# One hand-written issue order replaced by another in a fused adaLN, dilated local attention and token-MLP block

## The chip, the cores and the metric

The kernel runs on one core of a Trainium2 chip. The metric is device time in microseconds (us) of one execution. A second number appears in what follows: the span of the profiled execution, from the first instruction of the program to the end of the last, which is a little shorter than the time of the same execution.

## What is computed

x has 2048 positions of 512 numbers in bf16. Six rows come from a conditioning vector: shifts, scales and gates for two halves.

```python
sa, ca, ga, sb, cb, gb = rows of (silu(c) @ w_mod)            # 6 rows of 512
h = layernorm(x) * (1 + ca) + sa
x = x + ga * attention(h, A_wqkv, A_wo)
h = layernorm(x) * (1 + cb) + sb
x = x + gb * token_mlp(h)
# attention: 32 heads of 16; position s sees s, s-2, ..., s-14 (8 keys, dilation 2), softmax, then @ wo
# token_mlp: layernorm again, then gelu(h^T @ w1 + b1) @ w2 + b2 over the 2048 positions, F = 1792
```

The second half mixes positions: its first product sums over all 2048 positions, its second gives 2048 positions back.

## The kernel before

The positions are cut into 16 tiles of 128, and the tiles into five chunks of 2, 4, 4, 4 and 2 tiles (chunks 0 to 4). Every operation of the program is first recorded in a graph with a name, and then issued in an order that is written out by hand, the string ORDER. Its words are the names. A letter behind a name picks the engine where there are several: `a` ScalarE (ACT), `d` VectorE (DVE), `p` GpSimd (POOL), `s` the queue of SyncE (SP); `q` runs a matmul as four column strips of 32, `n` leaves out an optional extra matmul. `fill:n` issues n dummy 128-column matmuls. Each engine works through its own part of the list strictly in this order, and waits where an input is not there yet. A buffer from a pool (6 banks of PSUM, 4 `big` tiles for products, 5 `vD` tiles) goes to the operation that asks next in the list, and is the one that was freed earliest in the list, so the order also sets who waits for which buffer. All instructions carry the same line in the profile (L143, a wrapper), so groups are told apart by their tiles.

The names, for a chunk c and a tile t:

- `ld_...` are loads on the SP queue; `ld_x_4_14` brings tiles 14 and 15, `ld_wmod2` and `ld_wrow0..3` the weights of the conditioning rows, `ld_w1_...` and `ld_w2_...` those of the token MLP.
- `ln1s_t`, `ln1v_t`, `rstd1_c`, `nb1_c`, `n1_t`: statistics, reciprocal deviation, negative scaled mean (a tiny DVE operation) and norm of the first layernorm. The same with 2 and 3 in place of 1 for the second and third; there `ln2q_t` is the sum of squares on ACT, and `h3_t` is the third norm, which feeds the token MLP.
- `xt_t`: DMA transposes of two normed tiles for chunks 2 to 4.
- `wsc_k_j`: one quarter of a weight matrix scaled by 1 + ca, once. `qkv_c_kj` are the projections (k = 0, 1, 2 for q, k, v), and `ev_c_kj` moves a result out of PSUM to SBUF.
- `halo_v_c`, `halo_k_c` copy the last 16 positions of a chunk in front of the next.
- `qk_c_j` (DVE): elementwise products of q with the eight shifted k; `red_c_j` (PE) sums them over the head dimension into the PSUM tile psL. `max_c` (DVE), `sub_c` (PE), `exp_c` (ACT), `esum_c` (PE), `rcp_c` (ACT) and `smB_c` (DVE) are the softmax. `a2_c_j` and `vd_c_j` are DMAs that bring the weights and the shifted values in place. `pv_c_j` (DVE) multiplies them, `pvacc_c_j` (PE) sums, `oev_c_j` (ACT) brings the sum to SBUF.
- `wo_t` (PE): the output projection with x added; `x1_t` moves it to SBUF and sums it.
- `aff_t` (DVE): the second half's scale and shift, two instructions.
- `mlp1_l_f_s` (PE): pieces of the first token product for feature tile f from position tile s on, started before later tiles exist; `park_l_f` (ACT or DVE) puts a partial sum aside. `gelu_f` and `mlp2_t` follow, then `fin_t` and `st_out_t`.
- `modrow0`, `mrows0`, `st_row0`, `ld_row0` (and 1): the conditioning rows, sent through DRAM to be copied to all partitions; `woq_s` scales wo by ga.

What a step's DVE product looks like, and what the norms may run on:

```python
nc.vector.tensor_tensor(pv(), a2sb.unsqueeze(2).to_broadcast([P, 2, 4, C]), ..., op=ALU.mult)
G.add_any([("act", 0.8, lambda: nc.scalar.activation(dst, src, ACT.Identity, scale=r_, bias=n_)),
           ("dve", 0.42, lambda: nc.vector.tensor_scalar(dst, src, r_, n_, op0=ALU.mult, op1=ALU.add)),
           ("pool", 0.8, lambda: nc.gpsimd.tensor_scalar(dst, src, r_, n_, op0=ALU.mult, op1=ALU.add))],
```

The numbers in such a list were for the making of an order; with ORDER written out they set nothing.

Of the kernel before, what the change touches and what calls it, by code (L numbers as in the profile page):

```python
# [218 lines left out]
a2_3_0:s a2_3_1:s a2_3_3:s n2_4:a qkv4_00:q oev2_2:a rstd3_0 aff2 pvacc2_1 oev2_1:a wo6:q wo9:q wo7:q aff4 nb3_0  # L219
ln3s2:d ev4_02:a ln3s3:a ln3v3 h3_1:p wo8:q a2_3_2:s ev4_00:a ln3v2 ld_w2_0 ln3s4:d rstd3_2 x1_9:a ln3s5:a h3_0:p  # L220
mlp1_0_6_0:q x1_7:a ln3v4 x1_8:a h3_3 mlp1_0_1_0:q h3_2 mlp1_0_6_2:q mlp1_0_1_2:q pv3_1 mlp1_0_5_0:q ln3v5 ev4_10:a
ld_w1_0_896 x1_6:a mlp1_0_3_0:q mlp1_0_3_2:q ln2q7 pvacc3_1 rstd3_4 mlp1_0_5_2:q oev3_1:a mlp1_0_2_0:q pv3_0
mlp1_0_2_2:q nb3_4 h3_4:a mlp1_0_0_0:q mlp1_0_0_2:q h3_5:a mlp1_0_0_4:q qk4_0 ln2q8 ln2q6 park0_0:a ln2q9 mlp1_0_6_4:q
mlp1_0_2_4:q mlp1_0_1_4:q park0_1:a pv3_2 mlp1_0_5_4:q vd3_3 pvacc3_0 oev3_0:a mlp1_0_3_4:q ld_w2_1 park0_2:a pv3_3
red4_0 pvacc3_2 oev3_2:a mlp1_0_4_0:q qk4_1 pvacc3_3 ld_w1_0_1152 mlp1_0_4_2:q mlp1_0_4_4:q rstd2_6 oev3_3:a wo12:q
halo_v4:p vd4_2 vd4_3 nb2_6 n2_9:a qk4_2 n2_7:d qk4_3 wo10:qn red4_1 ld_w1_0_1408 n2_6:a vd4_1 n2_8:a aff6 red4_2
red4_3 max4 park0_3:a ln3s8:d ln3s6:d x1_12:a ln3v8 wo11 vd4_0 ln3s9:d mlp1_0_7_0 ld_w2_3 park0_4:a ln3v6 mlp1_0_7_2
park0_5:a ln3v9 x1_11:a ln2q12 mlp1_0_8_0 mlp1_0_8_2 park0_6:a wo13:n ln3s7:a ln3v7 sub4 mlp1_0_10_0 mlp1_0_9_0 x1_13:d
exp4 rstd3_6 nb3_6 esum4 mlp1_0_8_4 ln2q13 mlp1_0_10_2 mlp1_0_10_4 mlp1_0_9_2 rcp4 mlp1_0_7_4 h3_8:d rstd2_12
mlp1_0_12_0 mlp1_0_12_2 mlp1_0_12_4 smB4 a2_4_1:a a2_4_0:s mlp1_0_9_4 a2_4_2:s h3_9:d a2_4_3:a h3_7:d nb2_12 h3_6:p  # L230
mlp1_0_7_6 ln2q11 park0_7:a x1_10:d mlp1_0_8_6 ld_w1_0_1664 ln2q10 park0_8:a n2_13:p mlp1_0_9_6 park0_9:a n2_12:d aff12
rstd2_10 mlp1_0_10_6 park0_10:a ln3s13 pv4_2 nb2_10 ld_w1_1_0 pv4_1 mlp1_0_11_0 mlp1_0_11_2 mlp1_0_11_4 mlp1_0_12_6
pv4_0 mlp1_0_11_6 ld_w1_1_640 inj1_6:qn pv4_3 pvacc4_0 pvacc4_1 n2_11:a mlp1_0_13_0:q pvacc4_2 pvacc4_3 n2_10:a
mlp1_0_13_2:q park0_11:a mlp1_0_13_4 oev4_0:a oev4_2:a aff10 ln3s10:a wo14 inj1_3:n ln3s11:d ln3v11 x1_14 ln2s14 wo15
x1_15 mlp1_0_13_6 ln2v14 ln3s12 ln3v10 ln2s15 rstd2_14 nb2_14 ln2v15 n2_14:d rstd3_10 aff14 rstd2_15 nb2_15 inj1_4:qn
park0_12:a mlp1_1_3_6 park0_13:a mlp1_1_6_6 inj1_1:n mlp1_1_1_6 n2_15:p mlp1_1_4_6 inj1_0:n mlp1_1_0_6 nb3_10 h3_10:a
mlp1_1_4_10 mlp1_1_3_10 ln3s14:d ld_w2_4 mlp1_1_0_10 ln3v14 rstd3_12 h3_11:a mlp1_1_6_10 inj1_5:n mlp1_1_5_6
mlp1_1_5_10 rstd3_14 mlp1_1_1_10 aff15 nb3_12 ln3s15:d ln3v15 h3_12:p nb3_14 park1_0:+ h3_13:p rstd3_15 nb3_15 inj1_2:n
mlp1_1_2_6 ld_w1_1_896 h3_14:p h3_15:a ld_w1_2_0 park1_1:+ mlp1_1_2_10 park1_2:+ mlp1_1_7_10 park1_3:+ park1_4:+
park1_5:+ mlp1_1_8_10 mlp1_1_10_10 park1_6:+ padd1_7 padd1_10 gelu10 padd1_8 mlp1_1_9_10 padd1_9 gelu9 mlp1_2_4_11  # L240
mlp1_2_4_14 mlp1_2_1_11 mlp1_2_1_14 padd2_1 padd2_4 gelu7 mlp1_2_0_11 mlp1_2_0_14 padd2_0 gelu0 mlp1_2_2_11 gelu4 gelu8
mlp1_2_2_14 ld_w1_1_1408 mlp1_2_3_11 mlp1_2_3_14 padd2_3 gelu3 ld_w1_2_640 mlp1_2_6_11 padd2_6 gelu6 padd2_2 gelu2
mlp1_2_5_11 mlp1_1_11_10 padd1_11 mlp1_2_5_14 padd2_5 gelu1 gelu11 mlp1_1_12_10 ld_w2_5 ld_w2_7 mlp1_1_13_10 gelu5
mlp2_0_0 padd1_12 gelu12 mlp2_0_0b ld_w2_2 ld_w2_9 ld_w2_13 ld_w2_11 padd1_13 gelu13 mlp2_0_0c mlp2_6_0 mlp2_4_0 gsc
fin0_0 st_out0_0 fin4_0 st_out4_0 mlp2_8_0 fin8_0 mlp2_3_0 fin3_0 mlp2_2_0 fin2_0 st_out2_0 mlp2_1_0 fin1_0 mlp2_7_0
st_out3_0 fin6_0 st_out6_0 fin7_0 mlp2_10_0 fin10_0 st_out7_0 mlp2_11_0 mlp2_5_0 st_out1_0 fin5_0 st_out5_0 mlp2_14_0
fin11_0 st_out10_0 st_out11_0 ld_w2_15 fpre mlp2_9_0 mlp2_13_0 fin14_0 st_out14_0 st_out8_0 mlp2_12_0 fin9_0 st_out9_0
# [830 lines left out]
```

## Time and profile before

| what | us |
|---|---|
| median of 3 runs (lowest, highest) | 199.72 (199.3, 200.41) |
| the profiled execution | 199.64 |
| its span | 197.9 |
| granted TensorE clock, mean | 0.999 of full speed |

The page of the profile gives busy time by engine over the span, then groups of instructions. PE is TensorE's matmuls, PEld its weight loads, DVE is VectorE, ACT ScalarE, POOL GpSimd; SPq and ACTq are the sequencers of SP and ACT when they issue DMAs. A row of the timeline reads: start, duration, engine, line, operation, out<-in, shapes, count, and in brackets the engine's idle time before it and what ended it. Matmul ends are modelled, so TensorE can read busy while it works below its rate. Busy shares are means over stages with different limits, so the stages are looked at one by one.

### The profile page before, as it was taken

How to read it: one execution, taken by the hardware profiler on the slowest of the kernel's cores; microseconds unless marked ns; L12 is line 12 of the kernel's file. 1: busy time of each engine (PE TensorE's matmuls, PEld its weight loads, DVE VectorE, ACT ScalarE, POOL GpSimd, SP SyncE). 2: the span in 40 equal slices, each digit the busy share in tenths (PEclk: the TensorE clock that was granted, in tenths of full speed). 3: DMA queues.
4: the chain of work that ended last, by engine and by line, in shares of the span. 5: the costliest groups of instructions: out<-in, count | busy, mean ns of one | idle time of the engine just before them, and what ended most of it. 6: DMA issues, size and time to landing. Idle time of an engine off the chain costs nothing.

```text
span 197.9 us, 5606 instructions
## 1 busy us (share of the span) xinstructions
PE 187.8 (95%) x2348; PEld 101.9 (51%) x2358; DVE 157.5 (80%) x222; ACT 127.8 (65%) x305; POOL 18.5 (9%) x45
## 2 busy tenths in 40 slices
...
GB/s 171 325 358 321 219 227 164 156 57 260 230 223 285 236 191 215 105 159 298 40 332 227 76 209 143 156 241 233 329 224 325 74 0 53 39 44 53 172 53 53
DMA packets 53893, 36.02 MB, mean 182 GB/s; under 512 B 24428, under 2 KB 50668, under 8 KB 53868
## 3 DMA queue, kind: packets, MB, share of 16 engines
...
## 4 chain that ended last, share of the span: by engine, by line
PE 64%; ACT 19%; DVE 5%; DMA 4%; SPq 3%; issue 3%; ACTq 0%; DVEq 0%
PE psS L143 63%; ACT junk L143 4%; DMA vD<-v_sb 3%; SPq L143 3%; ACT xx L143 2%; ACT v_sb L143 2%; ACT h L143 2%; DVE big L143 2%; PE psL L143 2%; ACT q_sb L143 2%; ACT k_f L143 2%; DVE h L143 1%; ACT o_sb L143 1%; DMA c_t<-in_c_dram 1%; ACT lsb L143 1%
## 5 line engine op out<-in xcount | busy, mean ns | idle before, releaser
L143 PEld LDWEIGHTS <-wst 128*128 128x128 bf16 (+1 forms) x584 | 35.6, 101 | 33.0 <-issue 2.8
L143 PE MATMUL psS<-h,wst 128*32 128x512 bf16 (+1 forms) x358 | 50.5, 379 | 0.6 <-issue 0.2
L143 DVE TENSOR_TENSOR big<-q_sb,k_f 128x4096 bf16<-128x4096 bf16 (+1 forms) x20 | 36.6, 1857 | 0.1
L143 DVE TENSOR_TENSOR big<-a2sb,vD 128x4096 bf16<-128x4096 bf16 (+1 forms) x20 | 36.5, 1858 | 0.0
L143 PE MATMUL psS<-hT,w_qkv 128*32 128x512 bf16 (+1 forms) x576 | 29.6, 344 | 0.3 <-ACT o_sb L143 0.3
L143 DVE SCALAR_TENSOR_TENSOR h<-psS,bcol,rows_bc 128x512 f32<-128x512 f32 (+2 forms) x17 | 12.1, 710 | 22.1 <-PE psS L143 20.6
L143 PEld LDWEIGHTS <-w_qkv 128*32 128x32 bf16 (+1 forms) x618 | 22.1, 107 | 14.1 <-issue 0.5
L143 PE MATMUL psS<-gT,big 128*128 128x512 bf16 x110 | 24.7, 379 | 0.1
L143 PEld LDWEIGHTS <-big 128*128 128x128 bf16 x144 | 12.1, 98 | 13.8 <-DMA big<-in_w_mod_dram 0.5
L143 PE MATMUL psS<-woq,o_sb 128*32 128x512 bf16 (+1 forms) x207 | 16.7, 379 | 0.5 <-ACT o_sb L143 0.5
L143 ACT ACTIVATE gT<-psS,bcol 128x512 bf16<-128x512 f32 x14 | 9.0, 686 | 8.3 <-DVE psS L143 8.2
L143 POOL TENSOR_SCALAR h<-xx,rs,nb 128x512 bf16<-128x512 bf16 x9 | 7.0, 785 | 72.7 <-DVE nb L143 33.9
L143 DVE TENSOR_TENSOR psS<-psS,gT 128x512 f32<-128x512 f32 x14 | 9.3, 695 | 5.0 <-PE psS L143 5.0
L143 PE MATMUL psS<-hT,wst 128*32 128x512 bf16 (+2 forms) x135 | 11.7, 355 | 0.1
L143 ACT ACTIVATE h<-xx,nb,rs 128x512 bf16<-128x512 bf16 x15 | 11.6, 812 | 0.0
L143 DVE TENSOR_TENSOR h<-h,xx 128x512 bf16<-128x512 f32 (+2 forms) x17 | 11.1, 653 | 0.6
L143 PEld LDWEIGHTS <-group 128*32 128x32 bf16 x288 | 7.8, 96 | 7.2 <-issue 2.7
L143 DVE BATCH_NORM_STATS2 st<-xx 128x6 f32<-128x512 bf16 x12 | 8.0, 682 | 4.3 <-DMA xx<-in_A_x_dram 4.2
L143 DVE TENSOR_TENSOR h<-h,rows_bc 128x1024 bf16<-128x1024 bf16 (+2 forms) x16 | 10.9, 689 | 0.4
L143 ACT ACTIVATE junk<-xx,sums 128x512 bf16<-128x512 bf16 x14 | 10.1, 722 | 1.6 <-DVE xx L143 1.4
L143 ACT ACTIVATE v_sb<-psS,qvb 128x512 bf16<-128x512 f32 (+1 forms) x20 | 11.0, 597 | 0.0
L143 PEld LDWEIGHTS <-ident 128*32 128x32 bf16 (+2 forms) x242 | 7.1, 99 | 7.4 <-issue 2.8
...
## 6 DMA issues: line engine op xcount, KB each, us to landing
...
xx<-in_A_x_dram SPq DMA_DIRECT2D x6, 256.0 KB, 8.0
...
```

Of the source, the lines that this page charges most:

```text
L143: r = fn(*a, **k)
```

## The change

Only the string ORDER differs, from its 94th word on; the operations, their sizes and their operands stay. The set of names is the same. The engine changes for a few: `wsc2_0` goes from DVE to ACT; `n1_11`, `n1_14` and `n2_8` from ACT to POOL, `n2_1` from POOL to ACT; `h3_9` from DVE to ACT, `h3_6` from POOL to DVE, `n2_11` from ACT to DVE; `ln3s10` and `ln3s11` swap ACT and DVE; of the `a2` DMAs, `a2_0_2`, `a2_4_1` and `a2_4_3` go from ACT's queue to SP's, `a2_4_0` from SP's to ACT's. `qkv1_13`, `mlp1_0_7_0` and `wo11` become four strips, `qkv1_02`, `mlp1_0_1_0`, `mlp1_0_2_0` and `wo10` whole. Behind the common start the fillers were 1, 1, 18 and 14 dummy matmuls and are 6, 1, 2 and 4. All else is order. The first part, up to the start of the token MLP's first product, reads:

```diff
--- before
+++ after
@@ -196,57 +196,57 @@
-ln1s12:a ev0_02:d qkv1_13 ld_wqkv2 qkv0_20 ln1v13 qk0_3 qk0_2 ev1_13:a qk0_0 qvb1 ln1v12 qkv0_22:q ld_wrow0 red0_0
-ev1_00:a qkv1_03:q ev1_10:a qk0_1 red0_1 red0_2 red0_3 mask qvb_cp1:a ev0_20:a ev0_22:a wsc1_2:p halo_v1:a qk1_0
-ev1_03:a wsc1_3:a qkv1_11:q ld_wmod2 wsc2_3:a modrow0 ld_b1 mrows0:a ev1_11:a ld_wrow2 qkv1_02:q max0 wsc0_2:p ld_wo0
-n1_7:p sub0:q rstd1_3 qkv1_01:q ld_wo2 exp0 qkv1_12:q wsc1_1:p esum0:q qk1_3 red1_0 ev1_01:a qk1_1 ev1_02:a biascols:q
-n1_6:p ld_wrow1 rcp0 smB0 ev1_12:a ld_x_4_14 ln1s14 qkv1_22:q qk1_2 a2_0_2:a xt6 ld_wrow3 modrow1 red1_1 a2_0_1:a
-n1_9:p wsc2_0:d ln1s15 nb1_3 n1_11:a qkv1_23:q mrows1 qkv1_21:q ev1_21:a red1_2 red1_3 xt8 ev1_23:a fill:1:q n1_10:p
-qkv1_20:q ev1_20:a ev1_22:a qkv2_13:q qkv2_10:q wsc0_1:p vd0_2 ev2_13:a vd0_1 max1 sub1:q qkv2_00:q exp1 a2_0_0:s
-a2_0_3:s pv0_1 vd0_0 pv0_0 st_row0 pv0_2 qkv2_03:q esum1:q ld_wo3 pvacc0_0 vd0_3 halo_v2:p biascols_cp:a pvacc0_1 pv0_3
-pvacc0_2 pvacc0_3 ev2_10:a ev2_00:a qk2_0 n1_13:a n1_12:a ld_row0 woq_s rcp1 smB1 oev0_2:a qkv2_11:q qkv2_02:q ev2_03:a
-qk2_3 qkv2_01:q red2_0 oev0_0:a wo0:q wsc2_1:a wsc2_2:a qkv2_12:q ev2_11:a ev2_01:a ev2_02:a ev2_12:a wo1:q qkv2_21:q
-a2_1_1:a qkv2_22:q x1_1:a ln2q1 x1_0:a xt10 ln2q0 qk2_1 qkv2_23:q xt12 qk2_2 a2_1_0:s halo_k3:a vd1_2 a2_1_2:s
-qkv3_12:q a2_1_3:s pv1_2 rstd1_4 red2_1 nb1_4 vd1_0 st_row1 red2_2 red2_3 rstd2_0 ev2_22:a nb2_0 ev2_21:a qkv3_13:q
-ev3_13:a max2 vd1_3 pv1_0 n1_14:a vd1_1 pvacc1_2 n1_15:a qkv2_20:q ev2_20:a sub2:q qkv3_22:q ev3_12:a pv1_1 qkv3_10:q
-exp2 ev2_23:a halo_v3:a qkv3_20:q n2_0:a oev1_2:a ev3_10:a esum2:q rcp2 qkv3_00:q ev3_22:a qkv3_02:q ev3_00:a pv1_3
-ev3_02:a pvacc1_0 ev3_20:a qkv3_01:q ev3_01:a qkv3_11:q xt14 ld_row1 n2_1:p vd2_3 pvacc1_1 smB2 aff0 qk3_0 vd2_1
-fill:1:q vd2_0 oev1_0:a oev1_1:a pvacc1_3 ev3_11:a qk3_1 qkv3_23:q oev1_3:a a2_2_2:s ln3s1 qkv3_03:q wo4:q a2_2_1:s
-qk3_2 a2_2_0:s ev3_03:a ev3_23:a x1_4:a ln2q4 wo2:q x1_2:a a2_2_3:s red3_0 wo3:q x1_3:a ln2q3 qkv3_21:q ev3_21:a wo5:q
-red3_1 pv2_3 x1_5:a vd2_2 qk3_3 qkv4_20:q red3_2 qkv4_22:q red3_3 qkv4_12:q fill:18:q ln2q5 ld_w1_0_512 ln2q2 pv2_0
-pvacc2_0 vd3_0 ev4_20:a ln3s0 ev4_12:a rstd2_2 ev4_22:a qkv4_02:q oev2_0:a rstd2_4 nb2_2 n2_2:a max3 sub3:q exp3
-pvacc2_3 oev2_3:a qkv4_10:q pv2_2 vd3_2 esum3:q nb2_4 pv2_1 vd3_1 n2_3:p ld_w1_0_0 n2_5:a rcp3 smB3 pvacc2_2 fill:14:q
...
+ln1s12:a ev0_02:d ln1v13 qk0_2 qk0_0 qk0_1 qk0_3 ld_wqkv2 ld_wrow3 ld_x_4_14 qkv1_13:q qvb1 qkv0_20 ev1_10:a wsc2_2:a
+ev1_00:a ln1s14 ev1_13:a qkv1_03:q red0_0 qkv0_22:q ln1v12 rstd1_3 ev1_03:a qvb_cp1:a qkv1_11:q red0_1 red0_2 red0_3
+mask ld_wrow0 ld_wmod2 ld_wrow2 modrow0 qkv1_01:q ld_wrow1 ld_b1 qk1_0 max0 sub0:q qk1_3 ev0_20:a ev0_22:a ev1_11:a
+ev1_01:a exp0 wsc1_3:a halo_v1:a qkv1_12:q biascols:q qkv1_02 ev1_02:a esum0:q rcp0 mrows0:a ev1_12:a qk1_1 wsc0_1:p
+wsc1_1:p wsc0_2:p n1_7:p n1_9:p wsc1_2:p n1_6:p smB0 qk1_2 wsc2_3:a qkv1_22:q red1_0 qkv1_21:q modrow1 wsc2_0:a
+a2_0_1:a ev1_22:a ev1_21:a ln1s15 nb1_3 red1_1 qkv1_23:q red1_2 red1_3 mrows1 max1 xt6 xt8 qkv1_20:q ev1_23:a wsc2_1:a
+ev1_20:a qkv2_00:q qkv2_10:q vd0_2 vd0_3 vd0_1 ld_wo2 vd0_0 st_row0 a2_0_2:s a2_0_3:s a2_0_0:s ld_wo3 ld_row0 ld_wo0
+n1_11:p n1_10:p pv0_1 pv0_2 pv0_3 pv0_0 sub1:q ev2_00:a biascols_cp:a exp1 ev2_10:a qkv2_03:q pvacc0_2 qkv2_11:q
+fill:6:q qkv2_13:q esum1:q pvacc0_3 n1_12:a n1_13:a ev2_13:a ev2_03:a oev0_2:a pvacc0_0 pvacc0_1 rcp1 rstd1_4 oev0_0:a
+qk2_0 woq_s smB1 qk2_3 qkv2_01:q qkv2_12:q qkv2_02:q ev2_11:a ev2_01:a a2_1_1:a ev2_12:a ev2_02:a qk2_1 qk2_2 wo1:q
+x1_1:a wo0:q x1_0:a ln2q1 xt10 xt12 red2_0 qkv2_23:q qkv3_22:q qkv3_12:q vd1_0 st_row1 vd1_2 ev2_23:a ln2q0 rstd2_0
+nb1_4 nb2_0 qkv2_21:q ev2_21:a red2_1 a2_1_2:s a2_1_0:s a2_1_3:s vd1_1 ld_row1 vd1_3 n1_14:p pv1_2 qkv3_13:q red2_2
+red2_3 max2 qkv2_22:q n1_15:a ev3_13:a n2_1:a ev3_12:a ev2_22:a n2_0:a halo_v2:p qkv2_20:q sub2:q ev2_20:a exp2
+pvacc1_2 qkv3_10:q halo_v3:a oev1_2:a ev3_10:a qkv3_02:q qkv3_20:q pv1_1 qkv3_01:q pvacc1_1 esum2:q ev3_02:a ev3_20:a
+ev3_22:a aff0 pv1_0 qkv3_03:q qkv3_00:q pvacc1_0 pv1_3 oev1_1:a ev3_01:a rcp2 halo_k3:a smB2 ln3s0 qkv3_11:q oev1_0:a
+pvacc1_3 ev3_11:a oev1_3:a qkv3_23:q fill:1:q wo5:q wo3:q qk3_2 qk3_1 ld_w1_0_0 ld_w1_0_512 vd2_3 xt14 vd2_2 vd2_1
+a2_2_1:s a2_2_0:s a2_2_2:s vd2_0 a2_2_3:s wo4:q ln3s1 ev3_03:a ev3_00:a qk3_0 x1_3:a x1_4:a qk3_3 ln2q3 ln2q4 x1_5:a
+ev3_23:a qkv4_22:q qkv3_21:q ev3_21:a wo2:q red3_0 x1_2:a qkv4_20:q fill:2:q red3_1 qkv4_00:q red3_2 ev4_22:a ln2q5
+ln2q2 ev4_20:a rstd2_2 pv2_0 rstd2_4 red3_3 pvacc2_0 oev2_0:a pv2_3 qkv4_12:q ev4_12:a qkv4_02:q nb2_2 ev4_02:a n2_2:a
+max3 sub3:q pvacc2_3 exp3 esum3:q oev2_3:a rstd3_0 pv2_2 nb2_4 pvacc2_2 qkv4_10:q rcp3 n2_5:a oev2_2:a n2_4:a pv2_1
...
```

In the part left out the new list has, among others: `aff2 nb3_0 aff4 h3_1:p h3_0:p halo_v4:p ln3s3:a ln3s2:d ln3s4:d ln3v3 ln3v2 ln3v4 ln3s5:a ln3v5 pv3_1 ... h3_3 h3_2`, where the old one had `aff2 ... aff4 nb3_0 ln3s2:d ... h3_1:p ... h3_0:p ... h3_3 ... h3_2 ... pv3_1`; `x1_13` stands ahead of `qk4_3` and `aff6`; and the loads `ld_w2_0`, `ld_w2_4` and `ld_w2_2` have moved relative to the loads of w1. The last 16 output tiles are computed in another order of tiles.

More of the change, by code (lines that the diff above doesn't have):

```diff
@@ L218 @@
-pvacc2_3 oev2_3:a qkv4_10:q pv2_2 vd3_2 esum3:q nb2_4 pv2_1 vd3_1 n2_3:p ld_w1_0_0 n2_5:a rcp3 smB3 pvacc2_2 fill:14:q
[L219 to L247, printed above, removed]
@@ L248 @@
-fin13_0 st_out13_0 mlp2_15_0 fin12_0 st_out12_0 fin15_0 st_out15_0 mlp2_15_1 fin15_1 st_out15_1 mlp2_15_2 fin15_2
-st_out15_2
+ln1s12:a ev0_02:d ln1v13 qk0_2 qk0_0 qk0_1 qk0_3 ld_wqkv2 ld_wrow3 ld_x_4_14 qkv1_13:q qvb1 qkv0_20 ev1_10:a wsc2_2:a
+ev1_00:a ln1s14 ev1_13:a qkv1_03:q red0_0 qkv0_22:q ln1v12 rstd1_3 ev1_03:a qvb_cp1:a qkv1_11:q red0_1 red0_2 red0_3
+mask ld_wrow0 ld_wmod2 ld_wrow2 modrow0 qkv1_01:q ld_wrow1 ld_b1 qk1_0 max0 sub0:q qk1_3 ev0_20:a ev0_22:a ev1_11:a
+ev1_01:a exp0 wsc1_3:a halo_v1:a qkv1_12:q biascols:q qkv1_02 ev1_02:a esum0:q rcp0 mrows0:a ev1_12:a qk1_1 wsc0_1:p
```

31 lines of the change are left out of this document (added).

## The prediction

> **What bounds the kernel now.** I read the page's busy shares and chain first, then a table by stage, because the shares are means.
>
> ```profile
> PE 187.8 (95%) x2348; PEld 101.9 (51%) x2358; DVE 157.5 (80%) x222; ACT 127.8 (65%) x305; POOL 18.5 (9%) x45
> PE 64%; ACT 19%; DVE 5%; DMA 4%; SPq 3%; issue 3%; ACTq 0%; DVEq 0%
> ```
>
> The chain names TensorE for 64% of the span, and that is mostly its second half. The table by stage (columns after the stretch: its length, then busy time of PE, PEld, DVE, ACT, POOL with counts, granted clock, DMA share, GB/s) shows why:
>
> ```profile
> 15.00:75.00 60.00, 58.43 (x1240) 36.69 (x1243) 59.81 (x49) 56.07 (x131) 4.77 (x7) 1.00 0.75 214
> 75.00:76.00 1.00, 1.00 (x40) 0.82 (x36) 0.16 (x2) 0.97 (x4) 0.00 (x0) 1.00 0.03 8
> 76.00:94.00 18.00, 16.64 (x368) 9.14 (x360) 17.90 (x23) 17.61 (x47) 2.48 (x4) 1.00 0.77 205
> 94.00:146.00 52.00, 51.63 (x382) 24.25 (x380) 45.01 (x82) 41.11 (x98) 4.59 (x6) 1.00 0.76 204
> ```
>
> From 15 to 94 us DVE is busy for 59.81 of 60 us, then 0.16 of 1, then 17.90 of 18. ACT is nearly as full, and PE waits for both. From 94 us on PE itself is full, 51.63 of 52, and behind 146 us it has only the second token product left. The clock is full throughout. So the time is PE's work plus what PE loses ahead of 94 us. What it loses stands in its timeline:
>
> ```profile
> 72.81 0.61 PE L143 MATMUL psL<-big,group 128*32 128x512 bf16 x8 [0.67 <-DVE big L143]
> ...
> 74.11 1.16 PE L143 MATMUL psS<-ident 128*32 128x512 bf16 x24
> ...
> 77.19 0.62 PE L143 MATMUL psL<-m,nident 128*32 128x512 bf16 x8 [0.61 <-DVE m L143]
> ...
> 79.98 0.94 PE L143 MATMUL psS<-ident 128*32 128x512 bf16 x20
> ...
> 82.98 0.40 PE L143 MATMUL psS<-woq,o_sb 128*32 128x512 bf16 x4 [0.49 <-ACT o_sb L143]
> ```
>
> Two are dummy fillers (x24, x20), the rest waits for DVE and ACT: 0.67 + 1.16 + 0.61 + 0.94 + 0.49 = 3.9 us between 72 and 83 us, more than anywhere else. An order alone removes no PE work; it can only shorten this loss. As DVE has no idle time there but one microsecond, DVE's list decides.
>
> **The change part by part.** First, what leaves DVE before its last product of chunk 2 (`pv2_1`). I compared which DVE operations stand ahead of it in the old list and the new: the same ones but for `wsc2_0`. Beside that, DVE has one idle stretch.
>
> ```profile
> 32.15 0.35 DVE L143 TENSOR_SCALAR w_qkv<-h,a1col 128x512 bf16<-128x512 bf16 x1
> ...
> 33.38 1.22 DVE L143 TENSOR_REDUCE m<-psL 128x128 bf16<-128x1024 f32 x1
> ...
> 75.84 0.16 DVE L143 SCALAR_TENSOR_TENSOR nb<-sums,rs 128x2 f32<-128x2 f32 x1 [0.88 <-ACT rs L143]
> ...
> 79.32 2.29 DVE L143 TENSOR_TENSOR big<-a2sb,vD 128x4096 bf16<-128x4096 bf16 x1
> ```
>
> `wsc2_0` is the first row, 0.35 us. What follows soon is `max1`, the second row, and it also needs `red1_3` on PE:
>
> ```profile
> 32.29 1.05 PE L143 MATMUL psL<-big,group 128*32 128x512 bf16 x16
> ```
>
> That ends at 33.34, and `max1` began at 33.38. Its input `qk1_2` stays where it was, so only some 0.1 of the 0.35 comes through. The idle 0.88 us at 75 is `nb2_2` waiting for ACT's `rstd2_2`. In the new list ACT has `rstd2_2` behind `ev4_20` and ahead of `ev4_12`, and DVE reaches `nb2_2` a second earlier. Adding ACT's old durations in the new order, and its waits for PE, I get `rstd2_2` done near 74.2 and DVE there near 74.9. The stall goes. What is late next is `sub3`, then `exp3`. So `pv2_1`, which ended at 81.61, ends about 0.88 + 0.1 = 1.0 us earlier, less what a new wait takes:
>
> ```profile
> 30.06 1.34 SPq L143 DMA_DIRECT2D a2sb<-lsb  x2
> ...
> DMA to landing us min/median/max: 2.4/2.6/2.8
> ```
>
> SP issues one `a2_0` in 0.67 us (first row), and ACT's two landed in 2.4 to 2.8 (second row, from the view of the tile a2sb between 30 and 33 us). In the new list three of them stand on SP behind `vd0_0` and `st_row0`, so the last goes out near 32.0 and lands at 34.4 to 34.8, where `pv0_1` wants it at 34.4: 0 to 0.4 us, I take 0.2. `pv2_1` ends near 80.8, 0.8 us earlier.
>
> Second, from there to `wo6`, the matmul at 82.98. It waits for `oev2_1` on ACT.
>
> ```profile
> 78.05 1.00 ACT L143 ACTIVATE lsb<-psL 128x1024 bf16<-128x1024 f32 x1
> ...
> 82.33 0.60 ACT L143 ACTIVATE o_sb<-psS 128x512 bf16<-128x512 f32 x1
> 82.82 0.83 ACT L143 ACTIVATE q_sb<-psS,qvb 128x256 bf16<-128x256 f32 x2
> ```
>
> The first row is `exp3`, the second `oev2_1`. Between them ACT has 4.28 us of the same work in both lists, so `oev2_1` moves by what `exp3` moves. Ahead of `exp3` the new list has on ACT three more and three fewer, priced by three rows of the groups (count, busy us, mean ns, idle us before) and one of the timeline:
>
> ```profile
> L143 ACT ACTIVATE w_qkv<-wst,a1col 128x512 bf16<-128x512 bf16 x2 | 1.4, 709 | 0.0
> L143 ACT ACTIVATE h<-xx,nb,rs 128x512 bf16<-128x512 bf16 x15 | 11.6, 812 | 0.0
> L143 POOL TENSOR_SCALAR h<-xx,rs,nb 128x512 bf16<-128x512 bf16 x9 | 7.0, 785 | 72.7 <-DVE nb L143 33.9 <-PE psS L143 23.2 <-ACT junk L143 15.6
> 30.07 0.75 ACTq L143 DMA_DIRECT2D a2sb<-lsb  x1
> ```
>
> Added: `wsc2_0` 0.71, `n2_1` 0.81, `ev4_02` 0.83 (the row at 82.82) = 2.35. Removed: `n1_11` and `n1_14` to POOL, 2 x 0.81, and the issue of `a2_0_2`, 0.75 = 2.37. A wash. ACT gains only waits: 60 - 56.07 = 3.9 us not busy between 15 and 75, of which the issues of DMAs take some 1.5; the new list still meets waits at `x1_0`, `ev2_21` and the first `ev4_02`, some 1.5 us by the sums. I take 0.5 us for `exp3`, `oev2_1` and `wo6` (bounds: 0, if ACT's waits stay; 0.8, if all of DVE's gain passes). POOL has the room for the two norms: it is idle 72.7 us ahead of nine such norms, and `xt10` and `xt14`, which read them, stand on SP behind issues that go out later than they end.
>
> Third, behind `wo6` the sets of PE work are the same in both lists (only the order of `wo7` to `wo9` differs), so a gain at `wo6` stays unless PE waits anew. Weight loads show the old waits there:
>
> ```profile
> 89.11 0.31 PEld L143 LDWEIGHTS <-wst 128*32 128x32 bf16 x8 [0.41 <-issue]
> 89.69 0.55 PEld L143 LDWEIGHTS <-wst 128*32 128x32 bf16 x15 [0.27 <-issue]
> ...
> 93.76 1.20 PEld L143 LDWEIGHTS <-wst 128*32 128x32 bf16 x27 [0.45 <-issue]
> ```
>
> About 0.6 us beyond the normal spacing. In the new list `h3_3` and `h3_2` stand behind `pv3_1` instead of ahead of it.
>
> ```profile
> 86.69 0.70 DVE L143 TENSOR_SCALAR h<-h,mv,rs 128x512 bf16<-128x512 bf16 x2
> 87.31 2.28 DVE L143 TENSOR_TENSOR big<-a2sb,vD 128x4096 bf16<-128x4096 bf16 x1
> ```
>
> `pv3_1` then starts near 86.2 and the two norms end near 89.2. PE ends `wo9` near 86.8, has four pieces on tiles 0 and 1 (0.43 each) and `pvacc3_1`, and stands at 89.0: a wait of 0.2, and 0.3 for a bank that `ev4_10` frees. Later, `x1_13` (0.77) comes ahead of `aff6` on DVE and uses up the gain there, but PE has pieces to do. Cost against before: +0.1 (bounds -0.6 to +1.0).
>
> Fourth, the load `ld_x_4_14` takes the place of `ld_wmod2`, and its statistics `ln1s14` run on ACT near 20.5 instead of 28.84. Two rows of the timeline and one of the DMA issues (KB each, median us to landing):
>
> ```profile
> 12.59 0.37 SPq L143 DMA_DIRECT2D wst<-in_w_mod_dram  x1
> ...
> 18.88 1.01 SPq L143 DMA_DIRECT2D xx<-in_A_x_dram  x1
> xx<-in_A_x_dram SPq DMA_DIRECT2D x6, 256.0 KB, 8.0
> ```
>
> Issued at 12.59 and landing 8.0 us later, it is there at 20.6: a wait of 0.1. Bounds: 0, and 6.4 if it landed no sooner than before (18.88 + 8.0 = 26.9). The cover behind it is `ev1_12`, which ACT would end near 29.5 and DVE's `qk1_2` wants at 29.9. I take 0.
>
> **Sum**: -0.5 + 0.1 = -0.4 on the profiled execution of 199.64, so 199.24; that execution lies 0.08 below the median of the three runs, so **199.3** against 199.72.
>
> **The rivals.**
>
> *Faster.* If ACT follows DVE, 0.88 + 0.35 pass whole, and the 0.6 us of waits behind `wo6` go too: -1.8, 197.9. For it: the new list has 13 dummy matmuls behind the common start where the old has 34. Against it: ACT's sums above.
>
> *Slower: a tiny operation ahead of a big one on DVE.* The new list puts `nb1_4` and `nb2_0` ahead of `pv1_2`; the old one has them behind.
>
> ```profile
> 49.65 2.28 DVE L143 TENSOR_TENSOR big<-a2sb,vD 128x4096 bf16<-128x4096 bf16 x1
> 51.85 0.15 DVE L143 SCALAR_TENSOR_TENSOR nb<-mv,rs 128x2 f32<-128x2 f32 x1
> 51.93 0.15 DVE L143 SCALAR_TENSOR_TENSOR nb<-sums,rs 128x2 f32<-128x2 f32 x1
> 50.66 0.20 ACT L143 ACTIVATE rs<-lv 128x2 f32<-128x2 f32 x1
> ```
>
> `nb2_0` needs `rstd2_0`, the last row, done at 50.86. DVE gets there at 49.5 in the new list. By my sums `wo1` now precedes `wo0`, so `x1_1`, `x1_0`, both `ln2q` and `rstd2_0` are done near 49.2; the cover is 0.3 us. Past that, all of DVE stands, one for one, with `pv1_2`, `max2` and the whole of chunk 2 queued behind. If ACT is no earlier than before, it costs 50.86 - 49.5 = 1.4 us and with the gain lost at `exp3` as well (0.5) the sum is +1.5: **201.2**. It decides from a delay of 0.3 us in PE or ACT before 49 us.
>
> *About equal: POOL in DVE's way.* `nb3_0` now stands between `aff2` and `aff4`, so `h3_1` on POOL can start between the two halves of `aff4`.
>
> ```profile
> 37.72 0.38 POOL L143 COPY v_sb<-v_sb 128x64 bf16<-128x64 bf16 x1 [3.55 <-ACT lsb L143]
> 86.57 0.24 POOL L143 COPY v_sb<-v_sb 128x64 bf16<-128x64 bf16 x1
> ```
>
> The same copy took 0.38 us among DVE's products and 0.24 among its small operations: one of the two engines holds the other up. If the norm holds the second half of `aff4` for its 0.785 us, `pv3_1` and `h3_2` are later by as much, and PE loses it behind `wo9`: -0.4 + 0.8 = +0.4, 200.1. [...]
>
> **How the numbers follow.** The forecast, between 198.7 and 199.9, has 0.36; POOL at 200.1 0.10; faster at 197.9 0.22; slower at 201.2 0.32, since several covers of 0.1 to 0.5 us must all hold for the gain. A measurement of this kernel tells apart about 0.5%, 1.0 us: faster means below 198.7, slower above 200.7. Faster 0.23 and slower 0.34, with a little from the edges; within, 0.43. The range, 198.0 to 201.4, reaches to both outer cases; the forecast's own is 198.7 to 199.9.
>
> **What would show it.** Right: no idle time of DVE before `nb2_2`; `pv2_1` ending near 80.8; `wo6` near 82.5; PE full from 89 us, and the last stretch as long as before. Wrong: idle time of DVE at `nb2_0`, `pv0_1` or `qk1_2`; ACT waiting for xx near 20.5; `max1` later than 33.4; PE waiting for h3 behind `wo9` by more than 0.5 us; or a wait in the order of the last 16 output tiles, whose PE work is unchanged.

## The result, and the profile after

| what | before | after |
|---|---|---|
| median of 6 runs each (lowest, highest), us | 199.58 (199.3, 200.41) | 198.47 (198.32, 198.78) |
| ratio, 95% interval | | 0.9939 [0.9916, 0.9962] |
| the profiled execution, us | 199.64 | 198.75 |
| its span, us | 197.9 | 197.0 |

The new order is faster by 0.61%, 1.1 us; 0.4 us was forecast. The ratio is that of the means. The page of the new kernel has nearly the same busy times; POOL has 4.3 us more for one more instruction, and DVE's share of the chain rose from 5% to 21%:

```profile
PE 185.8 (94%) x2331; PEld 99.5 (50%) x2343; DVE 157.3 (80%) x222; ACT 127.1 (64%) x304; POOL 22.8 (12%) x46
PE 63%; DVE 21%; issue 5%; DMA 4%; SPq 3%; ACT 2%; DVEq 0%; ACTq 0%
```

The table by stage: DVE still has no room up to 94 us, and the microsecond at 75 us, where it was busy for 0.16, is now full. PE is full behind it, as before.

```profile
15.00:75.00 60.00, 59.50 (x1308) 36.90 (x1308) 59.47 (x50) 57.33 (x136) 6.46 (x7) 1.00 0.83 226
75.00:76.00 1.00, 0.16 (x8) 0.00 (x0) 1.00 (x2) 1.00 (x4) 0.77 (x1) 1.00 1.13 363
76.00:94.00 18.00, 15.70 (x299) 7.94 (x303) 17.80 (x23) 17.15 (x45) 2.44 (x3) 1.00 0.42 120
94.00:146.00 52.00, 51.63 (x393) 24.60 (x391) 45.31 (x84) 39.78 (x94) 5.53 (x6) 1.00 0.78 204
```

DVE's timeline, `max1`, `nb2_2` and `pv2_1`, each to be held against its row in the prediction. `nb2_2` has no idle time in brackets any more, and `pv2_1` starts at 78.34 in place of 79.32:

```profile
33.26 1.22 DVE L143 TENSOR_REDUCE m<-psL 128x128 bf16<-128x1024 f32 x1 [0.28 <-PE psL L143]
...
74.87 0.15 DVE L143 SCALAR_TENSOR_TENSOR nb<-sums,rs 128x2 f32<-128x2 f32 x1
...
78.34 2.28 DVE L143 TENSOR_TENSOR big<-a2sb,vD 128x4096 bf16<-128x4096 bf16 x1
```

ACT's timeline, `exp3` and `oev2_1`, and PE's, `wo6`: 1.09, 0.99 and 0.99 us earlier than before (78.05, 82.33, 82.98).

```profile
76.96 1.04 ACT L143 ACTIVATE lsb<-psL 128x1024 bf16<-128x1024 f32 x1
...
81.34 0.60 ACT L143 ACTIVATE o_sb<-psS 128x512 bf16<-128x512 f32 x1
```

```profile
81.99 0.83 PE L143 MATMUL psS<-woq,o_sb 128*32 128x512 bf16 x12 [0.27 <-ACT o_sb L143]
```

So all of the gain is there at `wo6`; the end of the profiled execution is 0.89 us earlier. What lies between adds up to nearly nothing, but it has three parts. First, POOL and DVE got in each other's way. POOL's timeline has `n1_14`, and `h3_1` with `h3_0`; DVE's has `aff4`:

```profile
49.96 2.76 POOL L143 TENSOR_SCALAR h<-xx,rs,nb 128x512 bf16<-128x512 bf16 x1 [16.09 <-ACT v_sb L143]
...
82.80 2.25 POOL L143 TENSOR_SCALAR h<-h,rs,nb 128x512 bf16<-128x512 bf16 x2 [6.85 <-ACT q_sb L143]
```

```profile
82.54 1.87 DVE L143 TENSOR_TENSOR h<-h,rows_bc 128x1024 bf16<-128x1024 bf16 x2
```

The two halves of `aff4` take 1.87 us where those of `aff2` take 1.41. From `wo6` to the weight load of `sub4` it is 22.67 us, before it was 22.49. Second, chunk 4 was better placed: on PE it is 13.40 us from the weight load of `sub4` (104.66) to that of `wo14` (118.06), before it was 13.83 (105.47, 119.30). Third, the end. DVE's last row and the queue's stores, after and then before:

```profile
192.07 2.75 SPq L143 DMA_DIRECT2D out_dram<-h  x6
...
193.65 0.29 DVE L143 TENSOR_TENSOR h<-psS,fpre 128x128 bf16<-128x128 f32 x1
```

```profile
193.30 2.39 SPq L143 DMA_DIRECT2D out_dram<-h  x4
...
194.89 0.29 DVE L143 TENSOR_TENSOR h<-psS,fpre 128x128 bf16<-128x128 f32 x1
```

The last addition ends at 193.94 and SP has issued all at 194.82, 0.88 later; before it was 195.18 and 195.69, 0.51. SP has six stores to issue in this last stretch where it had four. The three parts, +0.18, -0.43 and +0.37, add up to the 0.1 us that is lost behind `wo6`.

### The profile page after: what moved, and what is told of

Same layout as the page of the kernel before. It is cut to its first block, busy times and chain, and to the rows that moved or that the text cites. A ratio compares the mean times of both kernels' runs of the same rounds, so it can differ in the third digit from the quotient of the medians.

```text
span 197.0 us, 5568 instructions
## 1 busy us (share of the span) xinstructions
PE 185.8 (94%) x2331; PEld 99.5 (50%) x2343; DVE 157.3 (80%) x222; ACT 127.1 (64%) x304; POOL 22.8 (12%) x46
## 4 chain that ended last, share of the span: by engine, by line
PE 63%; DVE 21%; issue 5%; DMA 4%; SPq 3%; ACT 2%; DVEq 0%; ACTq 0%
PE psS L143 61%; DVE big L143 14%; DMA xx<-in_A_x_dram 4%; DVE h L143 4%; SPq L143 3%; PE psL L143 2%; DVE lsb L143 1%; DVE st L143 1%; ACT xx L143 1%; ACT junk L143 1%; DVE m L143 1%; DVE nb L143 0%; ACT k_f L143 0%; DVE woq L143 0%; ACT rs L143 0%
## 5 line engine op out<-in xcount | busy, mean ns | idle before, releaser
L143 PE MATMUL psS<-hT,w_qkv 128*32 128x512 bf16 (+1 forms) x576 | 29.0, 344 | 0.0
L143 PEld LDWEIGHTS <-w_qkv 128*32 128x32 bf16 (+1 forms) x618 | 21.2, 107 | 13.9
L143 POOL TENSOR_SCALAR h<-xx,rs,nb 128x512 bf16<-128x512 bf16 x11 | 11.5, 1047 | 94.3 <-DVE nb L143 40.6
L143 DVE TENSOR_TENSOR h<-h,rows_bc 128x1024 bf16<-128x1024 bf16 (+2 forms) x16 | 11.5, 718 | 0.5
L143 PE MATMUL psS<-big,group 128*32 128x512 bf16 (+1 forms) x160 | 9.9, 338 | 1.1 <-DVE big L143 0.8
L143 ACT ACTIVATE q_sb<-psS,qvb 128x512 bf16<-128x512 f32 (+1 forms) x18 | 10.6, 614 | 0.4 <-PE psS L143 0.3
L143 PEld LDWEIGHTS <-o_sb 128*32 128x32 bf16 (+1 forms) x220 | 7.0, 97 | 7.1 <-ACT o_sb L143 0.8
```

The source lines that it names most:

```text
L143: r = fn(*a, **k)
```

## The experiments

The first common steps start at times that differ by 0.9 us between executions (`ev0_10` at 15.51 to 16.40, and at 16.67 in run 8, whose edit lies ahead of it). The first loads land at other moments: in run 2 ACT waits 0.57 us for a load of x at 9.6 us, before it does not. So I compare distances within one trace, from the first copy of k (`ev0_10` on ACT) to the start of a step. For before and after these are its rows:

```profile
15.75 0.59 ACT L143 ACTIVATE k_f<-psS 128x512 bf16<-128x512 f32 x1
```

```profile
15.82 0.59 ACT L143 ACTIVATE k_f<-psS 128x512 bf16<-128x512 f32 x1
```

All runs, with the ratio of the means to before on the same chip (there its median was 199.56 to 199.63); `mlp2_0` is the first weight load of the second token product, behind which the PE work is the same everywhere.

| kernel | median, us | ratio [95%] | `pv2_1` | `exp3` | `pv3_1` | `mlp2_0` |
|---|---|---|---|---|---|---|
| before | 199.58 | 1 | 63.57 | 62.30 | 71.56 | 130.31 |
| after | 198.47 | 0.9939 [0.9916, 0.9962] | 62.52 | 61.14 | 70.40 | 129.00 |
| 1 old, `rstd2_2` early | 199.43 | 0.9989 [0.9974, 1.0004] | 62.60 | 62.50 | 71.25 | 130.07 |
| 2 old, fewer dummies | 200.71 | 1.0059 [1.0040, 1.0079] | 63.75 | 62.48 | 71.73 | 131.38 |
| 3 new to `wo6`, then old | 198.83 | 0.9962 [0.9938, 0.9985] | 62.36 | 60.97 | 70.33 | 129.08 |
| 4 old to `wo6`, then new | 205.23 | 1.0265 [1.0236, 1.0295] | 63.57 | 62.31 | 75.12 | 136.10 |
| 5 old, `halo_k3` late | 199.64 | 0.9979 [0.9951, 1.0008] | 63.47 | 62.20 | 71.45 | 130.20 |
| 6 old, two norms on POOL | 199.67 | 0.9996 [0.9972, 1.0020] | 63.73 | 62.46 | 71.72 | 130.46 |
| 7 new, `halo_k3` early | 199.57 | 0.9993 [0.9968, 1.0017] | 63.35 | 61.96 | 71.22 | 129.83 |
| 8 old, dummies at the start | 200.75 | 1.0042 [1.0016, 1.0067] | 63.52 | 62.25 | 71.50 | 130.24 |
| 9 old, ACT freed twice | 199.41 | 0.9991 [0.9976, 1.0005] | 63.41 | 62.14 | 71.40 | 130.15 |
| 10 new, two ends mended | 198.08 | 0.9928 [0.9903, 0.9952] | 62.42 | 61.04 | 69.95 | 128.56 |
| 11 new, `red2` first | 198.90 | 0.9970 [0.9956, 0.9985] | 62.74 | 61.55 | 70.62 | 129.23 |
| 12 new, more dummies | 198.55 | 0.9948 [0.9929, 0.9967] | 62.39 | 61.25 | 70.27 | 128.87 |

By this measure the new kernel is 1.05 us ahead at `pv2_1`, 1.16 at `exp3` and `pv3_1`, 1.31 at `mlp2_0`. Theory 1 was that DVE's wait of 0.88 us had gone and ACT had handed all of it on.

**1. Only DVE's wait taken away.**

```diff
-ln2q5 ld_w1_0_512 ln2q2 pv2_0 pvacc2_0 vd3_0 ev4_20:a ln3s0 ev4_12:a rstd2_2 ev4_22:a
+ln2q5 ld_w1_0_512 ln2q2 rstd2_2 pv2_0 pvacc2_0 vd3_0 ev4_20:a ln3s0 ev4_12:a ev4_22:a
```

> The old list with one name moved: `rstd2_2` directly behind `ln2q2`, ahead of `ev4_20` and `ev4_12` on ACT. Theory 1 (DVE's wait of 0.88 us at `nb2_2` was on the path and ACT hands it on whole): `nb2_2` finds no wait, `exp3` and `wo6` come 0.8 to 0.9 us earlier, 198.7 us. Rival A (ACT's own sums set `exp3`, as the prediction had it): the same operations stand ahead of `exp3`, so it stays within 0.2 us, 199.4 to 199.6. Rival B (the gain lies behind `wo6` or in the dummy matmuls): DVE is earlier, the time stays at 199.6.

DVE's `nb2_2` and ACT's `exp3` in this kernel:

```profile
74.67 0.15 DVE L143 SCALAR_TENSOR_TENSOR nb<-sums,rs 128x2 f32<-128x2 f32 x1
```

```profile
78.05 1.00 ACT L143 ACTIVATE lsb<-psL 128x1024 bf16<-128x1024 f32 x1
```

DVE is 0.97 us earlier at `pv2_1`, as in the new kernel, and ACT is not a bit earlier at `exp3` (+0.20). DVE then waits for ACT, at `smB3`:

```profile
80.78 0.69 DVE L143 TENSOR_TENSOR lsb<-lsb,rb 128x1024 bf16<-128x1024 bf16 x1 [0.35 <-ACT rb L143]
```

`mlp2_0` gains 0.24, and the interval of the times contains 1. Theory 1 falls; rival A, that ACT sets `exp3`, stands. An earlier DVE alone is not enough.

**2. Only fewer dummies.**

```diff
-fill:18:q
+fill:2:q
...
-fill:14:q
+fill:4:q
```

> The old list with 2 and 4 dummy matmuls where it had 18 and 14, as in the new list; nothing else. Rival B (dummy matmuls stood on the path): their 1.03 and 0.92 us shrink to 0.2 each and up to 1.6 us come through, 198.0 to 198.8. Theory 1 (they fill waits of PE for `pv2_1`): `wo6` starts within 0.1 us of before, 199.6.

Neither came: up to `exp3` the distance grows by 0.18, and then 0.9 us are lost in one place. DVE's timeline, at the first product of chunk 4 (`pv4_2`), and the kinds of DMA packets between 111 and 115 us (packets, MB, share of 16 engines):

```profile
115.27 1.23 DVE L143 TENSOR_TENSOR big<-a2sb,vD 128x2048 bf16<-128x2048 bf16 x1 [1.45 <-DMA a2sb<-lsb]
```

```profile
q8 instruction: 1, 0.02, 1.9%
```

One of the four `a2_4` transfers, issued 0.8 us later than in the old kernel, landed 2.4 us later, while a packet with 16 KB of instructions took 1.2 us of one DMA engine (1.9% of 16 engines' 4 us). In the old kernel a packet of that kind and size came at 107.6, ahead of the transfers. TensorE has 64 instructions fewer ahead: four dummies are issued as one matmul of 512 columns, so that 18 and 14 of them, in four strips, are 24 and 20 matmuls, 2 and 4 are 8 and 4, and each has a weight load. My explanation is that the packets with instructions therefore come at other moments; no view shows whose instructions they hold. Run 8 tries this.

**3. and 4. The halves apart.** The names that the first list has up to `wo6`, then all others in the order of the second list.

```diff
 fill:4:q oev2_1:a wo6:q
-wo7:q wo8:q wo9:q ev4_00:a smB3 n2_3:p vd3_3
+vd3_0 vd3_2 vd3_1 n2_3:p smB3 a2_3_0:s a2_3_1:s a2_3_3:s aff2 wo9:q wo7:q
...
```

```diff
 pvacc2_1 oev2_1:a wo6:q
-wo9:q wo7:q aff4 nb3_0 ln3s2:d ev4_02:a
+ev4_02:a wo7:q wo8:q wo9:q ev4_00:a vd3_3 ld_w1_0_896 a2_3_2:s ld_w2_1 nb3_0 aff4
...
```

> The new list up to `wo6`, and behind it all that is left in the old list's order. Theory 1 (the gain is made ahead of `wo6`; what lies behind it gains a further 0.25 us and loses 0.33 us at the last stores): `wo6` is 1.0 us early as in the new kernel and the time is 198.3 to 198.8. Rival C (the part behind `wo6` carries the gain): 199.3 or more.

> The old list up to `wo6`, and behind it all that is left in the new list's order. Theory 1: `wo6` as before, the time 199.4 to 199.9 (the later part's 0.25 us gained and the last stores' 0.33 us lost cancel). Rival C: 198.3 to 198.8.

Run 3 came as expected, though its median of 198.83 lies just above the range: `exp3` is as early as in the new kernel, and `mlp2_0` too. The gain is made ahead of `wo6`. Run 4 says nothing of the gain, as it made a new wait: `vd3_3` and the load `ld_w1_0_896` stand early in the new list's rest, and got between the transfers `a2_3_3` and `a2_3_2` on SP. DVE, `pv3_1`:

```profile
90.82 2.29 DVE L143 TENSOR_TENSOR big<-a2sb,vD 128x4096 bf16<-128x4096 bf16 x1 [3.35 <-DMA a2sb<-lsb]
```

**5. Only ACT's wait taken away.** Theory 2: ACT's own way to `exp3` sets the time. ACT's longest wait for DVE in the old kernel is at `halo_k3`, for `qk2_2` (the row of before):

```profile
49.76 0.26 ACT L143 ACTIVATE k_f<-k_f 128x64 bf16<-128x64 bf16 x1 [0.98 <-DVE big L143]
```

```diff
-xt12 qk2_2 a2_1_0:s halo_k3:a vd1_2 a2_1_2:s
+xt12 qk2_2 a2_1_0:s vd1_2 a2_1_2:s
...
-esum2:q rcp2 qkv3_00:q
+esum2:q rcp2 halo_k3:a qkv3_00:q
```

> The old list with one name moved: `halo_k3` (ACT, 0.26 us) from ahead of `rstd2_0` to behind `rcp2`, where the new list has it. ACT idles 0.98 us ahead of it in the old kernel, until DVE has ended `qk2_2`. Theory 2 (ACT's own stretch up to `exp3` sets the time, as the run before this one with `rstd2_2` moved showed): `exp3` comes 0.8 to 1.0 us earlier, and with it `wo6`: 198.6 to 198.9. Rival D (ACT waits later for what it gained): within 0.2 us of 199.6.

```profile
51.98 0.60 ACT L143 ACTIVATE k_f<-psS 128x512 bf16<-128x512 f32 x1 [0.90 <-PE psS L143]
```

Rival D came: the wait moved on to `ev3_13`, which needs `qkv3_13`, and that stands on PE behind `red2_2` and `red2_3`, which wait for the same `qk2_2`. `exp3` gains 0.10.

**6. Only less work for ACT.**

```diff
-n1_11:a
+n1_11:p
...
-n1_14:a
+n1_14:p
```

> The old list with two norms, `n1_11` and `n1_14`, on POOL in place of ACT, as in the new list; nothing moved. Theory 2: ACT's stretch up to `exp3` is shorter by 1.4 us, of which about 0.9 come through before DVE sets the pace: 198.5 to 198.8. [...]

ACT is relieved of 2 x 0.81 us and `exp3` is 0.16 later: ACT waits 0.39 at `exp1` and 0.26 at `ev2_20`, where it did not, and 0.48 at `x1_1` (0.17 before). The time is 199.67, not 198.5 to 198.8. Both norms took 0.77 us on POOL. DVE paid. Its `pv1_0` began while POOL was at a norm and took 2.63 us in place of 2.28 (DVE's timeline, then POOL's):

```profile
53.32 2.63 DVE L143 TENSOR_TENSOR big<-a2sb,vD 128x4096 bf16<-128x4096 bf16 x1
```

```profile
53.05 0.77 POOL L143 TENSOR_SCALAR h<-xx,rs,nb 128x512 bf16<-128x512 bf16 x1
```

The extra `n1_11` had also put POOL's scaling of a weight beside `pv0_1`, which took 1.47 in place of 1.22. By `smB2` DVE is 0.61 later than in the old kernel. So the run shows that two norms off ACT gain nothing in this list; it does not part ACT's relief from DVE's loss.

**7. The prediction's slower rival brought about.**

```diff
-ev2_23:a ln2q0 rstd2_0
+ev2_23:a ln2q0 halo_k3:a rstd2_0
...
-ev3_01:a rcp2 halo_k3:a smB2
+ev3_01:a rcp2 smB2
```

> The new list with `halo_k3` back ahead of `rstd2_0`. ACT then waits for the end of `qk2_2` (49.7 us) before `rstd2_0`, and `nb2_0` on DVE, ahead of `pv1_2`, waits for it: the prediction's slower rival, made on purpose. Theory 2 with that rival's price: DVE idles 0.8 to 1.1 us at `nb2_0`, all behind it is later by as much, 199.2 to 199.7. Rival D: DVE idles, but it is taken up ahead of `exp3`, 198.5 to 198.8.

ACT's `halo_k3`, DVE's `nb2_0`, and POOL's `n1_14` beside it:

```profile
49.41 0.26 ACT L143 ACTIVATE k_f<-k_f 128x64 bf16<-128x64 bf16 x1 [1.60 <-DVE big L143]
```

```profile
50.12 0.27 DVE L143 SCALAR_TENSOR_TENSOR nb<-sums,rs 128x2 f32<-128x2 f32 x1 [0.67 <-ACT rs L143]
```

```profile
49.61 0.77 POOL L143 TENSOR_SCALAR h<-xx,rs,nb 128x512 bf16<-128x512 bf16 x1 [15.94 <-issue]
```

DVE idles 0.67 us and all behind it is 0.83 later up to `mlp2_0`; the ratio gives back nearly all of the gain. What changes nothing in the old list is worth nearly all in the new one. ACT comes to `halo_k3` 0.9 us earlier than in the old list (from `ev0_10`) and waits 1.60 us there, in place of 0.98: what ACT gains ahead of 49 us is lost where it then waits for DVE.

**8. The dummies put elsewhere.**

```diff
-fill:4 cps
+fill:4 fill:16:q fill:10:q cps
...
-fill:18:q
+fill:2:q
...
-fill:14:q
+fill:4:q
```

> The old list with the dummy matmuls taken out behind the first part as in the earlier run (18 to 2, 14 to 4), and as many put in at the start, where TensorE waits for the first load: 26 in four strips, so that TensorE issues as many instructions in all as in the old kernel. Theory F (fewer dummies cost 1.1 us because the 16 KB fetches of instructions then fall at other moments, one of them on the transfers of a2 for chunk 4): the fetches stand where they stood, pv4_2 does not wait, 199.4 to 199.8. Rival G (the dummies at their place are needed, for the granted clock or otherwise): 200.3 to 200.9.

The time says rival G, the trace says theory F. From `ev0_10` on, all is as in the old kernel (-0.07 at `mlp2_0`), `pv4_2` does not wait, and the packet with instructions came at 108.0, with none between 111 and 115 us:

```profile
113.77 1.22 DVE L143 TENSOR_TENSOR big<-a2sb,vD 128x2048 bf16<-128x2048 bf16 x1
```

The loss is at the start (`ev0_10` at 16.67 in place of 15.75), and the edit made it: 33 dummy matmuls took 3.33 us there and delayed `cps` by 0.53 (4.70, before 4.17). Two of DVE's first norms then fell beside POOL's scalings of weights and took 0.79 and 0.78 us in place of 0.41. PE's timeline:

```profile
1.44 3.33 PE L143 MATMUL psS<-ident 128*128 128x512 bf16 x33 [1.44 <-POOL epscol L143]
4.70 0.17 PE L143 MATMUL psS<-ident,c_t 4*128 4x4 bf16 x1
```

**9. Both of ACT's waits taken away.** Theory 3: what ACT loses to `qk2_2` at 49 to 52 us, by whatever way, is the gain. As run 5, and `qkv3_13` ahead of `red2_2`.

```diff
-pv1_2 rstd1_4 red2_1 nb1_4 vd1_0 st_row1 red2_2 red2_3 rstd2_0 ev2_22:a nb2_0 ev2_21:a qkv3_13:q
+pv1_2 rstd1_4 red2_1 nb1_4 vd1_0 st_row1 qkv3_13:q red2_2 red2_3 rstd2_0 ev2_22:a nb2_0 ev2_21:a
```

> The old list with two names moved: `halo_k3` behind `rcp2` as in the run before, and `qkv3_13` (PE) ahead of `red2_2`, so that PE projects while DVE is still at `qk2_2`, as in the new list. Theory 3 (what ACT lost at 49 to 52 us, where it waited for DVE's `qk2_2` directly through `halo_k3` and then through `red2_2` and `qkv3_13`, is what the new order gains; from there to `exp3` ACT is full in both): `ev3_13` and all of ACT behind it come 0.6 to 0.9 us earlier, `exp3` near 77.3, 198.8 to 199.1. Rival H (another wait, for a bank of PSUM or for DVE at `nb2_2`, takes its place): within 0.2 us of 199.6.

```profile
50.84 0.60 ACT L143 ACTIVATE k_f<-psS 128x512 bf16<-128x512 f32 x1
52.15 1.52 ACT L143 ACTIVATE h<-xx,nb,rs 128x512 bf16<-128x512 bf16 x2 [0.71 <-DVE nb L143]
```

Rival H came. `ev3_13` no longer waits, and the next name does: `n1_14` needs `nb1_4`, which the old list has on DVE behind the product `pv1_2`. It is one wait in three places: 0.98, 0.90, 0.71 us.

**10. Two ends mended in the new list.**

```diff
-aff2 nb3_0 aff4 h3_1:p
+aff2 aff4 nb3_0 h3_1:p
...
-fin9_0 st_out9_0 fin11_0 fin14_0 st_out11_0 mlp2_13_0 fin13_0 st_out13_0 st_out12_0 st_out14_0
+fin9_0 st_out9_0 st_out12_0 fin11_0 fin14_0 st_out11_0 st_out14_0 mlp2_13_0 fin13_0 st_out13_0
```

> The new list with `nb3_0` back behind `aff4`, and `st_out12_0` and `st_out14_0` each directly behind the store that follows their own `fin` (`st_out9_0`, `st_out11_0`). Stores: the last three are issued 0.1 us behind `fin15_2` in place of 0.5, -0.35 us. `aff4`: if `h3_1` on POOL held it for 0.45 us and PE waits for what comes of it, -0.3 to -0.45 more: 197.7. Rival (PE has wo6 to wo9 to do meanwhile, so that the hold costs nothing): 198.1. If neither place was on the path: 198.5.

DVE (`aff2` and `aff4` in one row, and `pv3_1`), then the last stores beside DVE's last row:

```profile
81.14 2.74 DVE L143 TENSOR_TENSOR h<-h,rows_bc 128x1024 bf16<-128x1024 bf16 x4
...
85.87 2.29 DVE L143 TENSOR_TENSOR big<-a2sb,vD 128x4096 bf16<-128x4096 bf16 x1
```

```profile
191.72 2.44 SPq L143 DMA_DIRECT2D out_dram<-h  x4
...
193.31 0.29 DVE L143 TENSOR_TENSOR h<-psS,fpre 128x128 bf16<-128x128 f32 x1
```

`aff4` is back at 1.37 us, `pv3_1` is 0.45 earlier and `mlp2_0` 0.44: in this trace the hold had passed whole. The stores end 0.56 behind DVE in place of 0.88. The profiled execution is 198.09 against 198.75, 0.66 us, where 0.65 to 0.8 was expected. The times gain less, 0.2 us by the ratio and 0.4 by the medians, and 198.08 is the rival's 198.1, not 197.7. This is the fastest version, 0.72% ahead of before, but the times don't separate it from the new kernel, as the intervals overlap, so that the hold's price rests on the traces.

**11. `qkv3_13` behind the sums again, in the new list.**

```diff
-pv1_2 qkv3_13:q red2_2 red2_3
+pv1_2 red2_2 red2_3 qkv3_13:q
```

> The new list with `qkv3_13` on PE behind `red2_2` and `red2_3`, which wait for `qk2_2` on DVE (49.7 us). Theory 3: `ev3_13` comes 0.8 to 1.0 us later, ACT idles as long and is full from there to `exp3`, which is 0.6 to 1.0 us later: 199.1 to 199.5. Rival D (ACT takes it up before `exp3`): 198.4 to 198.7.

```profile
51.96 0.60 ACT L143 ACTIVATE k_f<-psS 128x512 bf16<-128x512 f32 x1 [1.03 <-PE psS L143]
```

The result lies between the two: ACT waits 1.03 us, `exp3` is 0.41 later, `mlp2_0` 0.23, and the ratio is higher by 0.003, 0.6 us, with intervals that just overlap.

**12. The old dummies in the new list.** Run 2 the other way round: 18 and 14 for 2 and 4.

```diff
-fill:2:q
+fill:18:q
...
-fill:4:q
+fill:14:q
```

> The new list with the dummy matmuls of the old one, 18 and 14 in place of 2 and 4. Theory 1 (they stand where PE waits for DVE and ACT): `wo6` within 0.1 us of the new kernel, 198.3 to 198.7. Rival B (the cut of the dummies is part of the gain): `wo6` 0.5 us later or more, 199.0 to 199.8. A change behind `wo6` alone would be neither, but a fetch of instructions that falls elsewhere.

There is no difference (-0.13 at `mlp2_0`): the cut of the dummies is no part of the gain.

## Why the prediction was right and where it missed

The measured 198.47 lies inside 198.0 to 201.4, and below the forecast's own 198.7 to 199.9: DVE's part came as described, ACT's was sized too small.

- **What bounds it**: half right. DVE is full up to 94 us before and after. But "DVE's list decides" is not so: in run 1 DVE was 0.97 us earlier at `pv2_1`, and `mlp2_0` 0.24.
- **DVE's term**: right in its mechanism, 0.99 us in place of 0.8. `rstd2_2` ended at 74.26 (74.2 forecast), and `nb2_2` began at 74.87 (74.9) without a wait. That alone was worth 0.97 (75.84 to 74.87). `max1` came 0.12 earlier (0.1), but nothing of it was left at `pv0_1`, which began at 34.55, before at 34.52: it waited 0.15 us for the `a2_0` transfers, where I had taken 0.2. Runs 3, 7, 10 and 11, with the same list up to there, do not have this wait. So `pv2_1` ended at 80.62, not 80.8.
- **ACT's term**: the mis-sized one. I took 0.5 us for ACT's waits, with 0.8 as the bound; `exp3` gained 1.09 and `wo6` 0.99. The bound was too low because DVE gained 0.99 and not 0.8. The operations were nearly the wash that I had added up; the waits that went were more than twice the 0.5 us. From `ev0_10` to `exp3` ACT (the fourth of the five) is busy for 58.31 of 62.30 us before and for 58.52 of 61.14 after, so its idle time fell by 1.4 us, from 3.99 to 2.62:

```profile
15.75:78.05 62.30, 60.12 (x1294) 37.62 (x1297) 61.27 (x51) 58.31 (x137) 4.79 (x7) 1.00 0.74 212
```

```profile
15.82:76.96 61.14, 59.59 (x1316) 36.52 (x1317) 60.61 (x50) 58.52 (x139) 6.42 (x7) 1.00 0.83 230
```

  In the old kernel 0.98 of the 3.99 stands at `halo_k3`, and 1.32 behind ACT's issues of `a2_0_2` and `a2_0_1`, of which the new list leaves ACT one; I had priced that at 0.75:

```profile
31.71 0.63 ACT L143 ACTIVATE junk<-xx 128x512 bf16<-128x512 bf16 x1 [1.32 <-issue]
```

  In the new kernel ACT's longest idle stretch is 0.52 us. No run moved `a2_0_2` alone; by run 7 what ACT gains there counts only if it does not wait for DVE at 49 us. For that the new list has three things at 49 to 52 us: `halo_k3` late, `qkv3_13` ahead of the sums, `nb1_4` ahead of `pv1_2`. Each leaves ACT free of DVE's `qk2_2` and `pv1_2` at another place. Put back alone, the first costs 0.83 us and the second 0.23 (runs 7 and 11); put into the old list, the first and the first two give 0.1 to 0.2 (runs 5 and 9). That all three together, with `rstd2_2` and `a2_0_2`, would bring the old list to the new time was not run: it is the likely rest, and not shown.
- **Behind `wo6`**: the sum was right by luck, its parts were not. The forecast was +0.1, and -0.99 at `wo6` became -0.89 at the end. `pv3_1` at 86.22 (86.2) and `h3_2` ending at 89.16 (89.2) came as forecast, but `aff4` lost 0.45, chunk 4 gained 0.43, and the last stores took 0.37 longer, where I had said "the last stretch as long as before".
- **The load `ld_x_4_14`**: right, ACT has no wait near 20.5.
- **The slower rival** did not come: `rstd2_0` was done at 48.68, 1.0 us before `nb2_0` began (49.72), not 0.3. Its mechanism is real (run 7), at 0.83 us instead of 1.4. **POOL in DVE's way** came, at 0.45 us instead of 0.8, beside a gain that was larger. **The faster rival** was closer than I gave it: ACT did gain as much as DVE. But ACT does not follow DVE (run 1), and the dummies have no part in it (run 12).
